# Two units to a matmul in the joins of 32-blocks, with G kept as its off-diagonal half

## Chip, cores, metric

One core of a Trainium2 chip. The time is the device time of the kernel in microseconds (us); each quoted time is a median of several executions. The kernel runs in fp32.

Words used below: PE is the matrix engine, DVE the vector engine, ACT the scalar engine, POOL the GpSimd engine. In this kernel PE's results go to PSUM; a copy or product that takes a result out of it is called an evacuation. Names that begin with ps are buffers in PSUM: psJ the joins, psG the Gram matrices, psK, psQ, psU, psY and psS the other small products of the recurrence, psT and psX transposes, psH and psO the feed-forward. In the profile every fp32 matmul is two instructions. The granted clock is the share of PE's full clock that the chip's throttle let through; half clock is 0.5.

## The reference, cut to what matters

A gated delta rule for 4 batches of 8 heads, 768 steps and head size 48, then a feed-forward block with exact GELU.

```python
for t in range(S):                                   # S = 768
    kt, vt, bt = k_n[:, :, t], v[:, :, t], beta[:, :, t, None]
    y[:, :, t] = einsum('bhd,bhde->bhe', q[:, :, t], state)
    v_old = einsum('bhde,bhd->bhe', state, kt)
    state = state + bt[..., None] * einsum('bhd,bhe->bhde', kt, vt - v_old)
h = y_as_rows @ w_in                                 # 3072 x 384 @ 384 x 2048
out = gelu_exact(h) @ w_out                          # 2048 x 384
```

## The kernel before

The recurrence runs in chunks of 64 steps. Two chunks make a group (there are six), and inside a group every 64x64 triangular system is solved in two steps: its two 32x32 diagonal blocks are inverted by elimination on DVE, for all 32 units (4 tiles of 8 heads) at once, and the off-diagonal 32x32 block then follows from two small products, the *joins* (level 0 and level 1). A unit has two halves p, in partitions 0-63 and 64-127. C is 64, HB is 32.

```python
def products(u, part=(0, 1)):                # Gram matrix of a chunk, 64x64 for each head
    ...
        nc.scalar.copy(heads(Gs[g][:, u.t]), psG[:, :, :, 0:C])          # G, whole, ACT
    ...                                                                  # P on DVE, from psG too
def pack(u, copy=nc.scalar.copy):            # the diagonal blocks in one piece, ACT
    ...
    copy(Ds[g][:, span], Gs[g][:, u.t, :, 0:HB])
    for p in range(2):                       # lower: partitions 32-63 of half p
        copy(Ds[g][lower, span], Gs[g][lower, u.t, :, HB:C])

def join(g, ts, level, copy=nc.scalar.copy):
    ...
    for i, u in enumerate(us):               # 16 units a call (8 in the start), p = 0 and 1
        for p in range(2):
            if level == 0:
                nc.tensor.matmul(psJ[low_, 0, col], lhsT=raw[top, u, HB:C],
                                 rhs=xm[top, u, :], start=True, stop=True)
            else:
                nc.tensor.matmul(psJ[top, 0, col], lhsT=xm[low_, u, :],
                                 rhs=zf[low_, u, HB:C], start=True, stop=True)
    for p in range(2):                       # two evacuations a call
        if level == 0:
            nc.vector.tensor_tensor(xm[low_, span, :], src, gm[...], op=ALU.mult)   # DVE
        else:
            copy(zf[top, span, HB:C], src)                                          # ACT
```

The start (group 0, first half) is scheduled by hand: elimination, joins, first solve. In the main part only DVE's order is fixed by hand; feed-forward matmuls (psH, psO) are laid between the small ones.

Of the kernel before, what the change touches and what calls it, by code (L numbers as in the profile page):

```python
# [8 lines left out]
F32 = mybir.dt.float32  # L9
U32 = mybir.dt.uint32  # L10
AX = mybir.AxisListType
ALU = mybir.AluOpType
# [4 lines left out]
def kernel(  # L17
# [28 lines left out]
    nc = tc.nc  # L46
    B, H, S, D = q.shape
    DM, DF = moe_w_in.shape
    C = 64
    HB = 32  # L50
    NC = S // C
    NP = H // 2
    NA = B // 2
    NG = NC // 2
    NU = 2 * NA * H
    NM = DM // 128
    NF = DF // 128
    HALF = [slice(0, C), slice(C, 2 * C)]
# [4 lines left out]
    wk = ctx.enter_context(tc.tile_pool(name="wk", bufs=2))  # L63
    ps = ctx.enter_context(tc.tile_pool(name="ps", bufs=2, space=bass.MemoryType.PSUM))
    start = ExitStack()
    su = start.enter_context(tc.tile_pool(name="su", bufs=2))

    def dn(name):
        return ps.tile([128, 2, 512], F32, tag="dn", name=name)
# [25 lines left out]
    for c in range(NC):  # L95
        for a in range(NA):
            u = tiles[c, a] = Unit()
# [53 lines left out]
    Zf = [cpool.tile([128, NU, C], F32, name=f"Zf{i}") for i in range(2)]  # L151
# [67 lines left out]
    Ds, Gs, Nus, XMs, gms, ns = {}, {}, {}, {}, {}, {}  # L219

    def heads(ap):
        return ap.rearrange("q (j r) d -> q r j d", r=2)
# [63 lines left out]
    def products(u, part=(0, 1)):  # L286
        g = u.c // 2
        cols = slice(part[0] * C, (part[-1] + 1) * C)
        psG = dn("psG").rearrange("q r (j n) -> q r j n", j=NP)
        for j in range(NP):  # L290
            for r, p in QUADS:
                rows = slice(r * C, r * C + D)
                nc.tensor.matmul(psG[HALF[p], r, j, cols], lhsT=u.KQt[rows, j, p, 0, :],  # L293
                                 rhs=u.KQt[rows, j, p].rearrange("q x n -> q (x n)")[:, cols],
                                 start=True, stop=True)
        if 0 in part:
            if u.t == 0:
                Gs[g] = wk.tile([128, 2 * NA, H, C], F32, tag="G", name="G", bufs=1)
            if u.t == 0 and g > 0:
                Ds[g] = wk.tile([128, NU, HB], F32, tag="diag", name="diag", bufs=1)  # L300
            nc.scalar.copy(heads(Gs[g][:, u.t]), psG[:, :, :, 0:C])  # L301
        if 1 in part:
            u.P = wk.tile([128, H, C], F32, tag="P", name="P", bufs=6)
            if u.c < 2:
                nc.scalar.copy(heads(u.P), psG[:, :, :, C:])
            else:
                nc.vector.tensor_tensor(heads(u.P), psG[:, :, :, C:], heads(mask_h), op=ALU.mult)  # L307

    def pack(u, copy=nc.scalar.copy):
        g = u.c // 2  # L310
        span = slice(u.t * H, (u.t + 1) * H)
        copy(Ds[g][:, span], Gs[g][:, u.t, :, 0:HB])
        for p in range(2):
            lower = slice(p * C + HB, (p + 1) * C)
            copy(Ds[g][lower, span], Gs[g][lower, u.t, :, HB:C])

    def masked(u, engine=nc.gpsimd):
        engine.tensor_tensor(u.P, u.P, mask_h, op=ALU.mult)

    def gram(u):  # L320
        products(u)
        pack(u)

    def diagonals(u):

# [13 lines left out]
    def eliminate_steps(g):  # L339
# [48 lines left out]
        steps += [(1.9, back, x) for x in range(3)]  # L388
        return steps

    def join(g, ts, level, copy=nc.scalar.copy):

        xm, zf, raw = XMs[g], Zf[g % 2], Gs[g].rearrange("q t h n -> q (t h) n")
        gm = gms[g].rearrange("q t h -> q (t h)")
        psJ = dn("psJ")
        us = range(ts[0] * H, (ts[-1] + 1) * H)
        span = slice(us[0], us[-1] + 1)
        for i, u in enumerate(us):
            for p in range(2):
                top = slice(p * C, p * C + HB)  # L400
                low_ = slice(p * C + HB, (p + 1) * C)
                col = slice(i * HB, (i + 1) * HB)
                if level == 0:
                    nc.tensor.matmul(psJ[low_, 0, col], lhsT=raw[top, u, HB:C],  # L404
                                     rhs=xm[top, u, :], start=True, stop=True)
                else:
                    nc.tensor.matmul(psJ[top, 0, col], lhsT=xm[low_, u, :],  # L407
                                     rhs=zf[low_, u, HB:C], start=True, stop=True)
        for p in range(2):
            top = slice(p * C, p * C + HB)  # L410
            low_ = slice(p * C + HB, (p + 1) * C)
            rows = top if level else low_
            src = psJ[rows, 0, 0:len(us) * HB].rearrange("q (u n) -> q u n", n=HB)
            if level == 0:
                nc.vector.tensor_tensor(  # L415
                    xm[low_, span, :], src,
                    gm[low_, span].unsqueeze(2).to_broadcast([HB, len(us), HB]), op=ALU.mult)
            else:
                copy(zf[top, span, HB:C], src)

    def gram_steps(c):
        us = [tiles[c, a] for a in range(NA)]
        return [(1.0, fn, u) for fn in (transposed, gram) for u in us]

    def v_steps(c):
        return [(1.0, scale_v, tiles[c, a], nc.vector if c == 2 else nc.gpsimd)
# [2 lines left out]
    def join_steps(g):  # L429
        return [(1.0, join, g, (2 * cc, 2 * cc + 1), level)  # L430
                for level in range(2) for cc in range(2)]
# [174 lines left out]
    for u in first:  # L606
        products(u, (0,))
    for u in first:
        transposed(u, (1,))
        products(u, (1,))  # L610
# [14 lines left out]
    for a in range(NA):  # L625
        join(0, (a,), 0)
    back2[0](*back2[1:])
    for a in range(NA):
        join(0, (a,), 1)
# [21 lines left out]
    def late():  # L651
        start.close()
        more = ctx.enter_context(tc.tile_pool(name="late", bufs=1))
        for i in range(4):
# [7 lines left out]
             at(1.02, 1.1, [(1.0, join, 0, (2, 3), level) for level in range(2)]),  # L662
]
    plan += [at(0.99, 1.0, [(1.0, prep, 2)]), at(1.055, 1.06, [(1.0, finish, 2)]), at(1.6, 1.61, [(1.0, finish, 3)]), at(2.75, 2.76, [(1.0, finish, 4)]), at(1.06, 1.14, gram_steps(2)),
             at(1.12, 1.6, state_steps(1)), at(1.5, 1.51, [(1.0, prep, 3)]),
             at(1.6, 1.75, gram_steps(3)), at(1.75, 2.45, eliminate_steps(1)),
             at(2.5, 2.62, join_steps(1)), at(2.62, 2.97, state_steps(2)),
             at(2.6, 2.61, [(1.0, prep, 4)]), at(2.65, 2.9, gram_steps(4))]
    plan += [at(1.62, 1.63, [(1.0, load, 4)]), at(0.995, 1.0, [(1.0, load_v, 2)])]
    plan += [at(c - 0.4, c - 0.3, v_steps(c)) for c in range(2, NC)]  # L670
# [46 lines left out]
```

## Time and profile before

| | before |
|---|---|
| time, median | 755.48 us (4 runs, 754.54 to 755.74) |
| PE busy | 704.0 us, 93% of the span |
| DVE busy | 376.4 us, 50% |
| ACT busy | 249.4 us, 33% |
| join call, steady part | 1.13 us of PE, 64 instructions |

The shares are averages over stages with different limits; the prediction tells the stages apart and shows the lines. In them the first two numbers of a timeline line are start and duration in us, and in a group's line the numbers after the first bar are busy us and mean ns of one instruction, after the second the idle time ahead of them and who ended it.

### The profile page before, as it was taken

What the parts mean: (1) busy time and instruction counts of PE and PEld (TensorE: products, weight loads), DVE (VectorE), ACT (ScalarE), POOL (GpSimd) and SP (SyncE); (2) the same over time, 40 slices, a digit from 0 to 9 for tenths busy, and PEclk for the clock granted to TensorE, in tenths of its full rate; (3) what the DMA queues carried; (4) which work ended last, traced back from release to release, by engine and by line L of the source; (5) the groups of instructions that cost most, each with busy time, mean ns of one, the idle gap of its engine ahead of it and who ended that gap; (6) DMA issues with size and microseconds to landing.
All of it is one profiled execution on the core that took longest, in us unless ns stands there. A gap on an engine that the chain in (4) does not pass through costs nothing.

```text
span 753.3 us, 19282 instructions
## 1 busy us (share of the span) xinstructions
PE 704.0 (93%) x8532; PEld 508.5 (68%) x8532; DVE 376.4 (50%) x855; ACT 249.4 (33%) x602; POOL 84.7 (11%) x91
## 2 busy tenths in 40 slices
PE   6549786899999999999999999999999999999997
PEld 5347553576687687687587687687687687586774
DVE  6988999996329722329822329822329821210100
ACT  3335633422553134352134352133352132122120
POOL 5051001203110002110012010012020010000000
PEclk9999999998999999999999999999999999999999
DMA  9807544400311101211101211001001000000000
GB/s 150 199 25 206 131 125 129 103 1 19 60 33 23 32 13 32 44 32 23 34 13 32 44 32 23 12 12 23 12 12 23 12 12 2 11 12 1 22 1 21
DMA packets 84515, 32.90 MB, mean 44 GB/s; under 512 B 77328, under 2 KB 80400, under 8 KB 84432
## 3 DMA queue, kind: packets, MB, share of 16 engines
q1 hardware_dynamic: 78384, 26.36, 16.0%
q10 hardware_dynamic: 5952, 5.12, 3.0%
q8 instruction: 67, 1.10, 0.6%
q0 software_dynamic: 96, 0.20, 0.1%
q14 instruction: 16, 0.13, 0.1%
HBM read 26.94 MB, written 4.72 MB: 42 GB/s over the span
## 4 chain that ended last, share of the span: by engine, by line
PE 77%; DVE 19%; issue 2%; DMA 1%; POOL 1%; ACT 0%; ACTq 0%; POOLq 0%; DVEq 0%
PE psO L544 30%; PE psH L535 30%; DVE tmp L359 3%; DVE Nu L361 3%; PE psT L283 2%; PE psG L293 2%; DVE w_e L204 2%; PE psU L470 2%; PE psJ L404 2%; PE psS L509 2%; PE psQ L447 2%; PE psK L447 2%; PE psJ L407 2%; PE psY L493 1%; DVE w_e L194 1%
## 5 line engine op out<-in xcount | busy, mean ns | idle before, releaser
L544 PE MATMUL psO<-w_out_sb,g 128*128 128x384 f32 x768 | 272.9, 500 | 10.2 <-DVE w_out_sb L205 10.2
L535 PE MATMUL psH<-xT,w_in_sb 128*128 128x256 f32 x1152 | 274.9, 388 | 3.4 <-DVE w_in_sb L205 3.0
L535 PEld LDWEIGHTS psH<-xT,w_in_sb 128*128 128x128 f32 x1152 | 213.1, 191 | 37.4 <-DVE w_in_sb L205 3.5
L544 PEld LDWEIGHTS psO<-w_out_sb,g 128*128 128x128 f32 x768 | 140.4, 192 | 97.2 <-DVE w_out_sb L205 15.6
L538 ACT ACTIVATE g<-psH 128x256 f32<-128x256 f32 x192 | 73.5, 383 | 177.4 <-PE psH L535 177.1
L361 DVE TENSOR_TENSOR Nu<-Nu,tmp 128x30 f32<-128x30 f32 (+9 forms) x180 | 61.9, 344 | 6.2
L359 DVE TENSOR_TENSOR tmp<-Nu 128x30 f32<-128x30 f32 (+9 forms) x180 | 61.8, 343 | 5.6
L253 POOL TENSOR_TENSOR n<-n,half 128x16 f32<-128x16 f32 x10 | 29.5, 2947 | 222.6 <-DVE n L242 222.6
L501 DVE TENSOR_TENSOR x<-psY,y 64x192 f32<-64x192 f32 x88 | 31.0, 353 | 42.3 <-PE psY L493 41.4
L307 DVE TENSOR_TENSOR P<-psG,mask 128x512 f32<-128x512 f32 x20 | 13.7, 690 | 72.8 <-ACT G L301 72.7
L512 DVE TENSOR_TENSOR St<-St,psS 128x384 f32<-128x384 f32 x22 | 12.2, 553 | 75.4 <-PE psS L509 75.0
L459 DVE TENSOR_TENSOR W<-psK,V 128x384 f32<-128x384 f32 x22 | 12.2, 555 | 73.6 <-PE psK L447 56.8
L475 ACT COPY U<-psU 64x192 f32<-64x192 f32 x92 | 28.8, 313 | 46.8 <-PE psU L470 46.0
L548 ACT COPY o_sb<-psO 128x384 f32<-128x384 f32 x24 | 11.5, 479 | 89.3 <-PE psO L544 89.3
L293 PE MATMUL psG<-KQt 48*64 48x128 f32 (+1 forms) x896 | 30.4, 286 | 3.9 <-ACT KQt L284 2.7
L522 ACT COPY xT<-psX 128x384 f32<-128x384 f32 x24 | 11.4, 477 | 68.0 <-PE psX L521 67.9
L293 PEld LDWEIGHTS psG<-KQt 48*64 48x64 f32 x896 | 24.9, 157 | 10.6 <-issue 4.8
L284 ACT COPY KQt<-psT 128x512 f32<-128x512 f32 x48 | 26.5, 589 | 9.1 <-PE psT L283 8.6
L383 POOL MEMSET Zf<- 32x512 f32 x23 | 12.2, 529 | 147.5 <-DVE Zf L374 145.5
L404 PE MATMUL psJ<-XM,G 32*32 32x32 f32 x768 | 15.5, 198 | 13.6 <-DVE XM L370 13.6
L415 DVE TENSOR_TENSOR XM<-psJ,gm 32x512 f32<-32x512 f32 (+1 forms) x26 | 16.9, 649 | 20.4 <-PE psJ L404 20.1
L196 ACT ACTIVATE w_e<-w_e,lim 128x384 uint32<-128x384 uint32 (+2 forms) x31 | 19.4, 625 | 23.0 <-DVE w_e L194 22.8
(100 smaller groups left out, 584.9 us busy)
## 6 DMA issues: line engine op xcount, KB each, us to landing
Qp<-in_q_dram SPq DMA_DIRECT2D x48, 96.0 KB, 3.4
V<-in_v_dram SPq DMA_DIRECT2D x48, 96.0 KB, 2.9
w_out_sb<-in_moe_w_in_dram SPq DMA_DIRECT2D x9, 512.0 KB, 5.3
out_dram<-o_sb ACTq DMA_DIRECT2D x48, 96.0 KB, 2.2
Zf<-in_moe_w_out_dram SPq DMA_DIRECT2D x8, 384.0 KB, 3.5
w_raw<-in_moe_w_out_dram SPq DMA_DIRECT2D x8, 384.0 KB, 3.1
Kp<-in_k_dram SPq DMA_DIRECT2D x28, 96.0 KB, 3.1
w_out_sb<-in_moe_w_in_dram SPq DMA_DIRECT2D x6, 256.0 KB, 4.4
```

Source lines behind the costliest of these rows:

```text
L253: nc.gpsimd.tensor_tensor(flat, flat, half, op=ALU.pow)
L284: nc.scalar.copy(u.KQt[:, :, :, x, :], psT.rearrange("q j (p n) -> q j p n", p=2))
L293: nc.tensor.matmul(psG[HALF[p], r, j, cols], lhsT=u.KQt[rows, j, p, 0, :], rhs=u.KQt[rows, j, p].rearrange("q x n -> q (x n)")[:, cols], s ...
L359: nc.vector.tensor_tensor(tmp, nu[:, j + 1:, j:j + 1].to_broadcast([128, n, j]), nu[:, j:j + 1, 0:j].to_broadcast([128, n, j]), op=ALU.mult)
L361: nc.vector.tensor_tensor(nu[:, j + 1:, 0:j], nu[:, j + 1:, 0:j], tmp, op=ALU.add)
L404: nc.tensor.matmul(psJ[low_, 0, col], lhsT=raw[top, u, HB:C], rhs=xm[top, u, :], start=True, stop=True)
L447: nc.tensor.matmul(psum(p, j, r), lhsT=u.KQt[rows, j, p, x, :], rhs=St[rows, u.a, p, j, :], start=True, stop=True)
L475: copies[i % len(copies)](pairs(u.U[HALF[p]], s), pairs(psU[HALF[p ^ s], p], s))
L501: nc.vector.tensor_tensor(dst, src, pairs(u.y[HALF[p ^ s]], s), op=ALU.add)
L535: nc.tensor.matmul(psH, lhsT=w_in_sb[:, m, f * 128:(f + 1) * 128], rhs=xTs[c][:, m, :], start=(m == 0), stop=(m == NM - 1))
L538: nc.scalar.activation(gs[f], psH, ACT.Gelu)
L544: nc.tensor.matmul(u.psO, lhsT=gs[f][:, u.a * 128:(u.a + 1) * 128], rhs=w_out_sb[:, f, :], start=(f == 0), stop=(f == NF - 1))
```

## The change

The intent: put two units side by side into one matmul, so that a join call has half as many. The weights are then 64 columns wide and the stream 64 columns long; the two 32x32 blocks on the diagonal of the 64x64 output are the wanted ones, the other two are waste. The two units' columns have to be merged into one weight operand, and the build refuses that when they do not lie side by side. So G is kept as its off-diagonal half alone and the diagonal blocks are copied straight from PSUM.

```diff
@@ products
-            nc.scalar.copy(heads(Gs[g][:, u.t]), psG[:, :, :, 0:C])
+            nc.scalar.copy(heads(Gs[g][:, span]), psG[:, :, :, HB:C])
+            if g > 0:
+                ...
+                nc.scalar.copy(heads(Ds[g][:, span]), psG[:, :, :, 0:HB])
+                for p in range(2):
+                    lower = slice(p * C + HB, (p + 1) * C)
+                    nc.scalar.copy(Ds[g][lower, span], Gs[g][lower, span])
... (pack and gram are gone)
@@ join
-        for i, u in enumerate(us):
+        for k in range(n):                       # n = half the units
             for p in range(2):
...
+                nc.tensor.matmul(psJ[HALF[p], k, :],
+                                 lhsT=left[rows, u:u + 2, :].rearrange("q u n -> q (u n)"),
+                                 rhs=right, start=True, stop=True)
         for p in range(2):
-            src = psJ[rows, 0, 0:len(us) * HB].rearrange("q (u n) -> q u n", n=HB)
+            for x in range(2):                   # four evacuations a call, half the size
+                src = psJ[p * C + x * HB:p * C + (x + 1) * HB, :, x * HB:(x + 1) * HB]
...
```

More of the change, by code (lines that the diff above doesn't have):

```diff
@@ L297, in products @@
             if u.t == 0:
-                Gs[g] = wk.tile([128, 2 * NA, H, C], F32, tag="G", name="G", bufs=1)
-            if u.t == 0 and g > 0:
-                Ds[g] = wk.tile([128, NU, HB], F32, tag="diag", name="diag", bufs=1)
-            nc.scalar.copy(heads(Gs[g][:, u.t]), psG[:, :, :, 0:C])
+                Gs[g] = wk.tile([128, NU, HB], F32, tag="G", name="G", bufs=1)
+            span = slice(u.t * H, (u.t + 1) * H)
+            nc.scalar.copy(heads(Gs[g][:, span]), psG[:, :, :, HB:C])
+            if g > 0:
+                if u.t == 0:
+                    Ds[g] = wk.tile([128, NU, HB], F32, tag="diag", name="diag", bufs=1)
+                nc.scalar.copy(heads(Ds[g][:, span]), psG[:, :, :, 0:HB])
+                for p in range(2):
+                    lower = slice(p * C + HB, (p + 1) * C)
+                    nc.scalar.copy(Ds[g][lower, span], Gs[g][lower, span])
         if 1 in part:
@@ L307, in products @@
                 nc.vector.tensor_tensor(heads(u.P), psG[:, :, :, C:], heads(mask_h), op=ALU.mult)
-    def pack(u, copy=nc.scalar.copy):
-        g = u.c // 2
-        span = slice(u.t * H, (u.t + 1) * H)
-        copy(Ds[g][:, span], Gs[g][:, u.t, :, 0:HB])
-        for p in range(2):
-            lower = slice(p * C + HB, (p + 1) * C)
-            copy(Ds[g][lower, span], Gs[g][lower, u.t, :, HB:C])
     def masked(u, engine=nc.gpsimd):
         engine.tensor_tensor(u.P, u.P, mask_h, op=ALU.mult)
-    def gram(u):
-        products(u)
-        pack(u)
     def diagonals(u):
@@ L389, in eliminate_steps, with every @@
         return steps
+    def every(ap, x):
+        return ap.rearrange("q (k x) n -> q k x n", x=2)[:, :, x]
     def join(g, ts, level, copy=nc.scalar.copy):
-        xm, zf, raw = XMs[g], Zf[g % 2], Gs[g].rearrange("q t h n -> q (t h) n")
+        xm, zf, off = XMs[g], Zf[g % 2], Gs[g]
         gm = gms[g].rearrange("q t h -> q (t h)")
-        psJ = dn("psJ")
-        us = range(ts[0] * H, (ts[-1] + 1) * H)
-        span = slice(us[0], us[-1] + 1)
-        for i, u in enumerate(us):
+        n = len(ts) * H // 2
+        psJ = dn("psJ")[:, 0, 0:n * C].rearrange("q (k n) -> q k n", n=C)
+        span = slice(ts[0] * H, (ts[-1] + 1) * H)
+        for k in range(n):
+            u = span.start + 2 * k
             for p in range(2):
@@ L401, in join @@
                 low_ = slice(p * C + HB, (p + 1) * C)
-                col = slice(i * HB, (i + 1) * HB)
                 if level == 0:
-                    nc.tensor.matmul(psJ[low_, 0, col], lhsT=raw[top, u, HB:C],
-                                     rhs=xm[top, u, :], start=True, stop=True)
-                else:
-                    nc.tensor.matmul(psJ[top, 0, col], lhsT=xm[low_, u, :],
-                                     rhs=zf[low_, u, HB:C], start=True, stop=True)
+                    rows, left, right = top, off, xm[top, u:u + 2, :]
+                else:
+                    rows, left, right = low_, xm, zf[low_, u:u + 2, HB:C]
+                nc.tensor.matmul(psJ[HALF[p], k, :],
+                                 lhsT=left[rows, u:u + 2, :].rearrange("q u n -> q (u n)"),
+                                 rhs=right, start=True, stop=True)
         for p in range(2):
@@ L411, in join @@
             low_ = slice(p * C + HB, (p + 1) * C)
-            rows = top if level else low_
-            src = psJ[rows, 0, 0:len(us) * HB].rearrange("q (u n) -> q u n", n=HB)
-            if level == 0:
-                nc.vector.tensor_tensor(
-                    xm[low_, span, :], src,
-                    gm[low_, span].unsqueeze(2).to_broadcast([HB, len(us), HB]), op=ALU.mult)
-            else:
-                copy(zf[top, span, HB:C], src)
+            for x in range(2):
+                src = psJ[p * C + x * HB:p * C + (x + 1) * HB, :, x * HB:(x + 1) * HB]
+                if level == 0:
+                    nc.vector.tensor_tensor(
+                        every(xm[low_, span, :], x), src,
+                        gm[low_, span].rearrange("q (k x) -> q k x", x=2)[:, :, x:x + 1]
+                        .to_broadcast([HB, n, HB]), op=ALU.mult)
+                else:
+                    copy(every(zf[top, span, HB:C], x), src)
     def gram_steps(c):
         us = [tiles[c, a] for a in range(NA)]
-        return [(1.0, fn, u) for fn in (transposed, gram) for u in us]
+        return [(1.0, fn, u) for fn in (transposed, products) for u in us]
     def v_steps(c):
```

## The prediction

> **What bounds the kernel now.** I read the page's slices first, then busy time by stage (windows), the chain of waits for each stage, the groups by shape, and last the starts of single matmuls in the trace.
>
> ```profile
> PE   6549786899999999999999999999999999999997
> DVE  6988999996329722329822329822329821210100
> ```
>
> Each digit is a slice of 18.8 us. Up to the ninth slice (about 170 us) DVE is nearly full and PE is not; after that PE is full. The windows say it in numbers (PE, PEld, DVE, ACT, POOL busy):
>
> ```profile
> 0.00:60.00 60.00, 33.20 (x882) 27.68 (x882) 47.41 (x123) 20.89 (x44) 19.48 (x34) 1.00 0.62 130
> 60.00:143.00 83.00, 67.78 (x778) 45.10 (x771) 79.75 (x176) 40.90 (x88) 8.52 (x8) 0.97 0.52 134
> 143.00:171.00 28.00, 26.14 (x129) 21.13 (x129) 25.66 (x67) 7.09 (x18) 1.92 (x1) 0.97 0.20 42
> 378.00:660.00 282.00, 281.59 (x3518) 203.36 (x3518) 112.50 (x248) 90.51 (x226) 27.41 (x24) 1.00 0.09 18
> ```
>
> So there are three regimes: a start in series (0 to 60 us), a DVE-bound stretch (79.75 of 83 us busy, then the elimination of group 1) and from 171 us a PE-bound stretch, in which only PE time counts. The chain of waits agrees: it runs through DVE lines to 170.7 us, then through PE without a hole. The change touches ACT copies (hidden in all three regimes: ACT is busy 90.5 of 282 us in the steady part), join matmuls (on the path from 171 us) and the joins' evacuations (on the path only in the start and the DVE stretch).
>
> The steady part, timeline of PE:
>
> ```profile
> 264.45 1.20 PE L404 MATMUL psJ<-XM,G 32*32 32x32 f32 x64
> 265.58 2.86 PE L535 MATMUL psH<-xT,w_in_sb 128*128 128x256 f32 x12
> 268.36 1.20 PE L404 MATMUL psJ<-XM,G 32*32 32x32 f32 x64
> 269.49 1.56 PE L535 MATMUL psH<-xT,w_in_sb 128*128 128x256 f32 x6
> 270.99 1.20 PE L407 MATMUL psJ<-Zf,XM 32*32 32x32 f32 x64
> 272.12 2.86 PE L535 MATMUL psH<-xT,w_in_sb 128*128 128x256 f32 x12
> ```
>
> A join call occupies PE from 264.45 to 265.58, 1.13 us for 64 instructions (32 matmuls; every fp32 matmul of this trace is two instructions). Feed-forward matmuls lie between a join and its use.
>
> **What the Trainium skill says.** (1) "TensorEngine Tiling (Array Packing)", Instruction Overhead: a matmul with one moving column has the same latency as one with 60. If that floor bound the joins, half the matmuls at twice the columns would halve their time. The trace disagrees: the psJ instructions start in pairs (one for each p, 6 or 7 ns apart), and pairs follow every 31.5 ns; 2 passes x 32 columns at 2.4 GHz are 26.7 ns. The pair is paced by its columns, not by a floor. (2) "TensorE: Matmul & The Clock Gate", LDWEIGHTS: the load takes a time set by its columns, not its rows. The trace agrees: psK (48 rows, 64 weight columns, 48 moving) starts its rounds of four every 58.8 ns, longer than 2 x 48 / 2.4 = 40 ns of streaming, and close to 2 x 64 / 2.4 = 53 ns of weights; psG with the same weights and 128 moving columns has rounds of 109 ns, and 2 x 128 / 2.4 = 107. So a round takes the longer of weights and stream, plus 2 to 5 ns. (3) "FP8 and Floating Point Precision", TensorE Precision Notes: true fp32 is four passes, which fits two instructions of two passes each.
>
> **The change, part by part.**
>
> *Join matmuls.* Two units side by side give 64 weight columns, 64 moving columns, 32 rows; half the output is waste. A call becomes 16 matmuls, 32 instructions, still in two tiles (p = 0 and 1), so 16 rounds instead of 32. By (1) and (2) each round is the larger of 53 ns (weights) and 53 ns (stream) plus about 5, call it 59 ns, against 31.5. First start to last: before 53 + 30 x 31.5 + 7 = 1.01 us (the trace: 1.009). After 95 (the first gap of psK is 93) + 14 x 59 + 7 = 0.93 us. From the last start to the next block's first: 121 ns for psJ (32 moving), 148 for psK (48), 199 for psG (128), hence about 158 for 64. The call: 0.93 + 0.16 = 1.09 instead of 1.13 us, 0.04 us less. On the PE-bound path lie 4 calls for each of five groups: 20 x 0.04 = 0.8 us. Group 1's calls partly run at half rate (pairs every 53 ns), where the same argument gives nothing more; I allow 0.1. **Minus 0.9 us.**
>
> *Evacuations of the joins.* Each becomes two of half the size. From the groups by shape:
>
> ```profile
> L415 DVE TENSOR_TENSOR XM<-psJ,gm 32x512 f32<-32x512 f32 x22 | 15.2, 690 | 20.3 <-PE psJ L404 20.1
> L415 DVE TENSOR_TENSOR XM<-psJ,gm 32x256 f32<-32x256 f32 x4 | 1.7, 424 | 0.1
> L419 ACT COPY Zf<-psJ 32x512 f32<-32x512 f32 x22 | 12.7, 575 | 19.2 <-PE psJ L407 19.0
> L419 ACT COPY Zf<-psJ 32x256 f32<-32x256 f32 x4 | 1.4, 362 | 0.1
> ```
>
> DVE: (690 - 424) / 256 = 1.04 ns an element and 158 ns fixed; ACT 0.83 and 149. So 2 x 690 becomes 4 x 424 on DVE (0.32 us more for a call), 2 x 575 becomes 4 x 362 on ACT. In the steady part both are hidden: psJ of level 0 ends at 265.6, its two evacuations end near 267, and level 1 reads them at 270.99, 4 us later. In the DVE-bound stretch one call (group 0, second half) pays: **plus 0.3 us.**
>
> In the start nothing hides them:
>
> ```profile
> 44.44 1.75 DVE L415 TENSOR_TENSOR XM<-psJ,gm 32x256 f32<-32x256 f32 x4
> 46.23 1.93 DVE L374 STREAM_TRANSPOSE Zf<-Nu 128x1024 f32<-128x1024 f32 x1
> 48.26 0.63 ACT L381 ACTIVATE Zf<-low 32x512 f32<-32x512 f32 x1 [16.57 <-DVE Zf L374]
> 48.90 1.49 ACT L419 COPY Zf<-psJ 32x256 f32<-32x256 f32 x4
> 49.73 1.96 PE L470 MATMUL psU<-W,Zf 64*64 64x48 f32 x64 [2.32 <-DVE w_in_sb L197]
> ```
>
> This is a series: four DVE products, the transpose, the zeroing on ACT, two of the four copies (they end at 49.63), then psU. Its stated releaser is a DVE line, but psU starts 0.1 us after the second copy and reads what it writes. Four products of 0.437 us pitch (1.75) become eight of 128 elements: 158 + 133 = 291 ns, pitch about 0.31, 2.45 us: plus 0.7. Two copies (0.74) become four of 149 + 106 = 255 ns, pitch 0.27, 1.07 us: plus 0.33. **Plus 1.0 us** for everything behind. The join matmuls of the start are slower there (pairs of 53 ns) and finish under the second transpose, 42.5 to 44.4; twice the columns in half the rounds keeps that.
>
> *Gram copies.* A unit from chunk 2 on costs ACT 584 (G) + 404 + 2 x 402 (diag, the small ones being 32 partitions) = 1.79 us; afterwards two PSUM reads of 256 columns, 372 each (the psD copy of the same shape), and 2 x 402 = 1.55 us. That is 0.24 x 20 = 4.8 us of ACT, and 0.84 us in the four units of group 0, but no wait in the chain ends on these copies except 1.9 us in all before the flip transposes, and there the POOL product with the scales (143.29 to 145.21) ends after the transpose anyway. **0 us.** The freed half of G (4 KB in each partition) is not missing anywhere.
>
> Sum: 1.0 + 0.3 - 0.9 = +0.4 us on 755.7, so **756.1 us**.
>
> **Rivals.** (a) The joins are bound by instruction count: 1.13 would become about 0.62 us, 20 x 0.5 = 10 us less, 745. For it: 17.7 ns an instruction is the lowest pitch of any group, and psK with its 32 instructions occupies 0.61 us. Against it: the 31.5 ns rounds of two, while psG and psK issue four in 20 ns. (b) The two wide tiles no longer run together (64 weight columns for 32 rows occur nowhere in this trace): 32 x 56 ns = 1.8 us a call, plus 0.7 x 20 = 14 us, 769. For it: only that the shape is new; against it: four 64-column tiles run together in psK, and p = 0 and 1 share no rows and no output partitions. (c) The four evacuations hold back level 1 or the next user of psJ's buffer: the slack of 4 us speaks against it; if it were a wait of 0.5 us at 20 calls, 766. (d) The main part fixes by hand only DVE's order, so other durations can move ACT and PE work against each other; that is worth a few us either way, and I cannot work it out.
>
> **Range and chances.** The sum is made of terms of at most 1 us, runs of before spread over 1.2 us, and (d) adds perhaps 2 to 3 us: 753.0 to 759.5. To leave 2% the time must move by 15 us: (a) falls short of it, (b) just misses. Faster 0.01, same 0.97, slower 0.02.
>
> **What would show it.** Right: join calls at 1.05 to 1.12 us in the steady part, rounds of two near 58 ns; psU at 50.6 to 50.9 instead of 49.73 and group 1's first join about 1.3 us after 170.7; the end less than 1 us after that of before. Wrong: join calls near 0.6 or 1.8 us (rivals a, b), idle PE before psJ of level 1 (c), or a different order of PE blocks between 171 and 707 us (d).

## The result and the profile after

The changed kernel took 756.61 us (median of 4 runs, 756.29 to 756.78), predicted 756.1. Ratios here are the mean time of one kernel's fast runs over the mean of the other's in the same rounds, so they are not quite the ratio of the medians; for this one it is 1.0017 (95% interval 0.9999 to 1.0034). In a second set with more rounds it was 1.0021 (0.9999 to 1.0043). Both intervals still hold no change at all, so the times alone do not size an effect this small. All outputs are right.

Where the trace of the changed kernel stands against that of the kernel before (starts in us, read from the timelines):

| event | before | changed | shift |
|---|---|---|---|
| XM transpose that ends the first elimination | 40.57 | 41.00 | +0.43 |
| first psU | 49.73 | 51.13 | +1.40 |
| first psH | 60.06 | 61.66 | +1.59 |
| elimination of group 1 begins | 142.95 | 145.48 | +2.54 |
| first join of group 1 | 170.70 | 173.22 | +2.52 |
| psK after the joins of group 1 | 181.15 | 183.07 | +1.93 |
| first join of group 5 | 605.09 | 606.57 | +1.48 |
| end | 753.30 | 754.57 | +1.27 |

The start and the DVE-bound stretch lose 2.5 us; 0.6 us come back between the first join of group 1 and the psK after it, and 0.66 us from there to the end. The 0.6 us cannot be put down to the joins: over all traces this piece takes 9.90 to 10.45 us with old joins (the kernel before, kernels 2 and 8 below) and 9.85 to 10.20 us with new ones (the changed kernel twice, kernel 1). Half clock falls into it. In the kernel before it began 1.25 us after the first join and lay on a busy PE all the time; in the changed kernel its first 0.93 us fell on an idle PE.

**The joins in the steady part.** PE's timeline, changed kernel:

```profile
266.38 1.15 PE L406 MATMUL psJ<-XM,G 32*64 32x64 f32 x32
267.45 2.86 PE L536 MATMUL psH<-xT,w_in_sb 128*128 128x256 f32 x12
270.24 1.15 PE L406 MATMUL psJ<-XM,G 32*64 32x64 f32 x32
271.32 1.56 PE L536 MATMUL psH<-xT,w_in_sb 128*128 128x256 f32 x6
```

Half the instructions (x32), nearly the same time: from a call's first start to the next block's first start it is 1.077 us, before 1.130. The pairs of instructions (p = 0 and 1) start every 58.4 ns instead of every 31.7.

**The evacuations.** Groups by shape, changed kernel:

```profile
L415 DVE TENSOR_TENSOR XM<-psJ,gm 32x256 f32<-32x256 f32 x44 | 18.5, 421 | 18.9 <-PE psJ L406 18.4
L420 ACT COPY Zf<-psJ 32x256 f32<-32x256 f32 x44 | 16.0, 363 | 19.2 <-PE psJ L406 18.7
L415 DVE TENSOR_TENSOR XM<-psJ,gm 32x128 f32<-32x128 f32 x8 | 2.3, 288 | 0.1
L420 ACT COPY Zf<-psJ 32x128 f32<-32x128 f32 x8 | 2.0, 256 | 0.1
```

Twice as many, at 421 and 288 ns on DVE instead of 690 and 424, so each halving costs what the fixed part of an instruction costs. In the start that shows, all engines' timeline of the changed kernel (lines between left out):

```profile
44.87 2.42 DVE L415 TENSOR_TENSOR XM<-psJ,gm 32x128 f32<-32x128 f32 x8
47.31 1.92 DVE L368 STREAM_TRANSPOSE Zf<-Nu 128x1024 f32<-128x1024 f32 x1
49.33 0.63 ACT L375 ACTIVATE Zf<-low 32x512 f32<-32x512 f32 x1 [16.40 <-DVE Zf L368]
49.97 2.14 ACT L420 COPY Zf<-psJ 32x128 f32<-32x128 f32 x8
51.13 2.14 PE L471 MATMUL psU<-W,Zf 64*64 64x48 f32 x64 [2.58 <-ACT Zf L420]
```

The eight products take 2.42 us where four took 1.75, and psU starts 1.16 us after the first copy instead of 0.83. Its releaser is now named as the ACT copy, which fits the reading that the DVE releaser named before was only the last semaphore seen.

**The DVE-bound stretch** lost 0.95 us (from +1.59 to +2.54), of which two more evacuations (four of 0.42 for two of 0.69) explain 0.3. Most of the rest is one wait. DVE's timeline, first the kernel before, then the changed one:

```profile
95.73 0.69 DVE L205 SCALAR_TENSOR_TENSOR w_in_sb<-w_in_sb,w_e 128x512 f32<-128x512 f32 x1
96.34 0.68 DVE L204 SCALAR_TENSOR_TENSOR w_e<-w_out_sb,w_e 128x512 uint32<-128x512 uint32 x1
```

```profile
97.65 0.69 DVE L205 SCALAR_TENSOR_TENSOR w_in_sb<-w_in_sb,w_e 128x512 f32<-128x512 f32 x1
98.90 0.69 DVE L204 SCALAR_TENSOR_TENSOR w_e<-w_out_sb,w_e 128x512 uint32<-128x512 uint32 x1 [0.56 <-ACT w_e L196]
```

DVE waits 0.56 us for an ACT step of the weight decoding. In ACT's timeline copies that wait for PE stand ahead of that step. So the question is why PE was late. The windows point to its clock (PE, PEld, DVE, ACT, POOL busy in us; then the mean granted clock of PE, here the number after the last bracket), kernel before, then changed:

```profile
80.00:83.00 3.00, 3.00 (x37) 2.08 (x37) 2.93 (x7) 1.38 (x3) 0.00 (x0) 0.50 0.93 230
83.00:87.00 4.00, 4.00 (x54) 2.96 (x54) 3.83 (x8) 1.93 (x5) 0.00 (x0) 0.97 0.81 105
```

```profile
80.00:83.00 3.00, 1.46 (x4) 1.17 (x4) 2.93 (x7) 0.21 (x1) 0.00 (x0) 0.52 0.46 120
83.00:87.00 4.00, 4.00 (x40) 2.79 (x38) 3.86 (x8) 1.17 (x3) 0.00 (x0) 0.51 1.16 214
```

In both kernels PE falls to half clock near 80 us, before for 3.4 us, in this run of the changed kernel for 6.8 us (the clock records of the trace give the lengths). Whether that belongs to the change is a question for the experiments.

**The gram copies** left a trace that I had not predicted. DVE's mask product P reads the same PSUM tile as ACT's copies and waits for them; from the page of each kernel, before and then changed:

```profile
L307 DVE TENSOR_TENSOR P<-psG,mask 128x512 f32<-128x512 f32 x20 | 13.7, 690 | 72.8 <-ACT G L301 72.7
```

```profile
L313 DVE TENSOR_TENSOR P<-psG,mask 128x512 f32<-128x512 f32 x20 | 13.7, 690 | 73.5 <-ACT diag L304 73.5
```

It now waits for the second of two copies of 256 columns (370 and 377 ns, overlapping a little), which ends about 0.06 us later than the one copy of 512 (584 ns). Behind P on DVE come the products x, and PE waits for those before one transpose; PE's timeline, before and then changed:

```profile
319.36 0.55 PE L521 MATMUL psX<-ident,x 128*128 128x128 f32 x3 [0.21 <-DVE x L501]
```

```profile
321.14 0.55 PE L522 MATMUL psX<-ident,x 128*128 128x128 f32 x3 [0.27 <-DVE x L502]
```

This occurs in three of the groups: 3 x 0.06 = 0.2 us. It closes the account of the steady part: 16 calls x 0.053 = 0.85 us won, 0.2 lost, 0.65 net; from psK to the end the table has 1.93 - 1.27 = 0.66.

### The profile page after: what moved, and what is told of

Same layout as the page of the kernel before. It is cut to its first block, busy times and chain, and to the rows that moved or that the text cites. A ratio compares the mean times of both kernels' runs of the same rounds, so it can differ in the third digit from the quotient of the medians.

```text
span 754.6 us, 17817 instructions
## 1 busy us (share of the span) xinstructions
PE 703.3 (93%) x7764; PEld 507.9 (67%) x7764; DVE 381.0 (50%) x881; ACT 245.8 (33%) x628; POOL 84.4 (11%) x91
## 4 chain that ended last, share of the span: by engine, by line
PE 78%; DVE 17%; issue 1%; ACT 1%; DMA 1%; SPq 0%; POOL 0%; ACTq 0%; DVEq 0%; POOLq 0%
PE psH L536 30%; PE psO L545 30%; PE psJ L406 3%; DVE tmp L353 3%; DVE Nu L355 3%; PE psT L283 2%; PE psU L471 2%; PE psG L293 2%; PE psQ L448 2%; PE psK L448 2%; PE psS L510 2%; DVE w_e L204 2%; PE psY L494 1%; DVE w_out_sb L199 1%; PE psX L522 1%
## 5 line engine op out<-in xcount | busy, mean ns | idle before, releaser
L415 DVE TENSOR_TENSOR XM<-psJ,gm 32x256 f32<-32x256 f32 (+1 forms) x52 | 20.8, 401 | 19.1 <-PE psJ L406 18.4
L406 PE MATMUL psJ<-XM,G 32*64 32x64 f32 x384 | 16.0, 243 | 14.1 <-DVE XM L364 14.1
```

Of the source, the lines that this page charges most:

```text
L406: nc.tensor.matmul(psJ[HALF[p], k, :], lhsT=left[rows, u:u + 2, :].rearrange("q u n -> q (u n)"), rhs=right, start=True, stop=True)
```

## The experiments

Theory: a round of matmuls (one in each tile that works at the time; a tile here is a block of PE's rows and columns that holds one small weight matrix) takes the longer of its weight load and its stream, so wide matmuls save almost nothing; the start pays for halved evacuations; the rest is small. Eight kernels were run, in two sets of four, each set beside its own runs of the kernel before (11 runs, median 755.55 us in the first set, 753.69 in the second; why these differ is found below).

### 1. The start undone

```diff
@@ start only; join_one is the join of before, on the new G
-        join(0, (a,), 0)
+        join_one(0, (a,), 0)
...
-        join(0, (a,), 1)
+        join_one(0, (a,), 1)
```

> The changed kernel, but the four join calls of the start (group 0, first half) again with one unit to a matmul and two evacuations a call. My theory: the start pays about 1.0 us for the halved evacuations, nothing else of it changes, so psU starts about 1.0 us earlier than in the changed kernel and the time is about 755.6 us (1.0 below the changed kernel's 756.6). Rival (the halved evacuations cost nothing, the longer start comes from other order or from waits before the joins): no change, 756.6 us.

Measured: 755.23 us (5 runs, 754.69 to 756.42), ratio to before 1.0002 (0.9989 to 1.0014). PE's timeline:

```profile
49.55 1.96 PE L501 MATMUL psU<-W,Zf 64*64 64x48 f32 x64 [2.33 <-DVE w_in_sb L197]
```

From the first XM transpose to psU it is 9.17 us, as in the kernel before (9.16) and not as in the changed kernel (10.13). The rival falls. A steady join call still takes 1.077 us.

### 2. The gram copies alone

```diff
@@ from the changed kernel: every join as before, on the new G (in short; join's whole body is replaced)
-    def join(...)      # two units to a matmul
+    def join(...)      # one unit to a matmul, two evacuations, lhsT=off[top, u, :]
```

> Only the gram copies of the change (G kept as its off-diagonal half, diagonal blocks copied straight from PSUM); all joins with one unit to a matmul and two evacuations. My theory: ACT busy falls by about 5.6 us to some 244, nothing on the path moves: 755.5 us, within 0.4 of the kernel before. Rival (the new ACT durations move waits: the 0.4 us that psD waits in the start of the changed kernel and the 0.6 us that DVE waits there for ACT's decode near 98 us): 756.3 to 756.6 us.

Measured: 754.75 us (5 runs, 754.45 to 756.93), ratio 0.9999 (0.9985 to 1.0014). ACT busy fell by 7.0 us to 242.4, more than I had worked out. The lines behind it, groups by shape of this run:

```profile
L300 ACT COPY G<-psG 128x256 f32<-128x256 f32 x24 | 8.9, 371 | 31.5 <-PE psG L293 31.5
L304 ACT COPY diag<-psG 128x256 f32<-128x256 f32 x20 | 7.6, 378 | 0.0
```

Two PSUM reads of 256 columns stand in place of one of 512 and one SBUF copy. The durations of all these copies sum to 5.6 us less than before (38.2 to 32.6), as worked out; neighbouring ones now also overlap, by 2.0 us in all, and ACT's other work took 0.6 us more. In the time, nothing shows (the interval allows about 1 us either way), and DVE does not wait near 97 us in this trace, so the rival finds no support; what that wait goes with is found below. But psX waits 0.27 us at 319 us here as well, and from psK to the end this run loses 0.18 us to the trace of before, the 0.2 us of the account above. So the gram copies cost about 0.2 us by the traces (0.3 in kernel 8, which has them and the old joins there too); the timing cannot resolve it.

### 3. Four tiles at once

```diff
@@ join, from kernel 1: one unit to a matmul again, x = 0, 1 go to different column groups
-            for p in range(2):
+            for x, p in ((0, 0), (0, 1), (1, 0), (1, 1)):
...
-                nc.tensor.matmul(psJ[HALF[p], k, :],
-                                 lhsT=left[rows, u:u + 2, :].rearrange("q u n -> q (u n)"),
-                                 rhs=right, start=True, stop=True)
+                nc.tensor.matmul(psJ[p * C + x * HB:p * C + (x + 1) * HB, k, 0:HB],
+                                 lhsT=left[rows, u + x, :], rhs=right[:, x, :],
+                                 start=True, stop=True)
...
-                src = psJ[p * C + x * HB:p * C + (x + 1) * HB, :, x * HB:(x + 1) * HB]
+                src = psJ[p * C + x * HB:p * C + (x + 1) * HB, :, 0:HB]
```

> Start as before; in all other join calls one unit to a matmul (32 weight columns, 32 moving), but the two units of a pair write to different column groups, so that four 32x32 tiles work at once; 64 instructions a call as before the change, four half-size evacuations as in the change. My theory (a round is paced by 2 x 32 columns, 31.5 ns, however many tiles are in it): 16 rounds, a call takes 53 + 14 x 31.5 + 20 + 121 = 0.64 us instead of 1.13 (before) and 1.08 (changed), so 20 x 0.44 = 9 us below the first run of this set, about 747 us. Rival (the count of instructions binds, 17.7 ns each): a call stays at 1.13 us, about 756.5 us.

Measured: 749.13 us (6 runs, 746.31 to 750.29), ratio 0.9917 (0.9899 to 0.9936). PE's timeline:

```profile
264.81 0.75 PE L406 MATMUL psJ<-XM,G 32*32 32x32 f32 x64
265.50 2.86 PE L566 MATMUL psH<-xT,w_in_sb 128*128 128x256 f32 x12
```

The same 64 instructions of the same shape as before the change, in 0.682 us a call instead of 1.130: the count of instructions does not bind, the number of tiles at work does. The gain was smaller than expected (6.1 us below kernel 1 by the medians, not 9). A call was 0.04 us longer than worked out, because after the first half of it the starts no longer come in fours every 31.7 ns but in twos every 17 ns; so the 16 calls of groups 2 to 5 give 6.3 us. And group 1's four, partly at half clock, gave almost nothing (9.95 us from its first join to psK, 10.20 in kernel 1).

### 4. Wide weights, narrow stream

```diff
@@ join, from kernel 1: 32 matmuls a call, x and p as in kernel 3
+                wide = left[rows, u:u + 2, :].rearrange("q u n -> q (u n)")
+                nc.tensor.matmul(psJ[HALF[p], k, x * HB:(x + 1) * HB], lhsT=wide,
+                                 rhs=right[:, x, :], start=True, stop=True)
```

> Start as before; in all other calls the weights are two units wide (64 columns) but each matmul streams only one unit (32 columns), 32 matmuls a call, two tiles a round. My theory (a round takes the longer of weights and stream): rounds of 59 ns set by the weights, a call 95 + 30 x 59 + 7 + 121 = 2.0 us, 20 x 0.92 = 18 us above the first run of this set, about 774 us. Rival (only the stream paces a round, the weights are hidden): rounds of 31.5 ns, a call 1.13 us, about 756.7 us.

Measured: 777.01 us (4 runs, 775.88 to 780.61), ratio 1.0296 (1.0274 to 1.0318). PE's timeline:

```profile
276.15 2.05 PE L407 MATMUL psJ<-XM,G 32*64 32x32 f32 x64
278.14 2.86 PE L566 MATMUL psH<-xT,w_in_sb 128*128 128x256 f32 x12
```

The stream is that of the kernel before, only the weights are wide, and a call takes 1.98 us; pairs start every 58.4 ns, as in the changed kernel. So 64 weight columns alone set that pace. The profiled run is the slowest one (780.61 us, 6.6 above expectation), and 6 us of that lie in group 1: there PE ran at half clock for 23.9 us (6.8 in the kernel before), and the four calls took 14.0 us together instead of about 8. Why the other three runs (775.88 to 777.33) lie 2 to 3 us above expectation no trace shows.

### 5. Narrow weights, wide stream

```diff
@@ join, from kernel 1: 32 matmuls a call, four tiles as in kernel 3
+                nc.tensor.matmul(psJ[p * C + x * HB:p * C + (x + 1) * HB, k, :],
+                                 lhsT=left[rows, u + x, :], rhs=right,
+                                 start=True, stop=True)
```

> The mirror of the run with wide weights: start as before; in all other calls the weights are one unit (32 columns), each matmul streams two units (64 columns), the two units of a pair in different column groups (four tiles a round, 64 instructions a call). My theory (a round takes the longer of weights and stream): rounds of four at 59 ns set by the stream, a call 1.08 us as in the changed kernel, time as in the run with only the start undone, about 755.5 us. Rival (the weights alone made the changed kernel's rounds long, the stream is hidden): rounds as in the four-tile run, a call 0.68 us, about 749 us.

Measured: 756.65 us (4 runs, 755.56 to 757.10), ratio 1.0027 (1.0007 to 1.0046). PE's timeline:

```profile
266.44 1.09 PE L406 MATMUL psJ<-XM,G 32*32 32x64 f32 x64
267.46 2.86 PE L566 MATMUL psH<-xT,w_in_sb 128*128 128x256 f32 x12
```

Rounds of four start every 56 ns, a call takes 1.03 us against 0.68 with the narrow stream. So 64 streamed columns alone also set nearly that pace. Kernels 4 and 5 together show "the longer of the two": both wide together (the changed kernel, 58.4 ns) is no slower than the weights alone, and either one was enough to take back what the halved count gave. The time missed its forecast by 1.1 us, although the calls were shorter than forecast; in the profiled run group 1 took 12.4 us from its first join to psK (10.2 in kernel 1), with half clock for 10.2 us in place of 6.8.

### 6. Four tiles, group 0 as before

```diff
@@ plan, from kernel 3
-             at(1.02, 1.1, [(1.0, join, 0, (2, 3), level) for level in range(2)]),
+             at(1.02, 1.1, [(1.0, join_one, 0, (2, 3), level) for level in range(2)]),
```

> The four-tile kernel, but all joins of group 0 (start and second half, in the DVE-bound stretch) with one unit and two evacuations as before. Two theories of the 0.9 to 1.6 us by which the DVE-bound stretch was longer in all runs with the new joins there: (A) it is the new join at 63 to 70 us: 0.3 us of evacuation, and a PE that is a little less busy there, so that the half-clock stretch at 80 us lasts 6.8 to 10.2 us instead of 3.4 and DVE waits for ACT near 97 us; then this run has one 3.4 us half-clock stretch there and starts the elimination of group 1 within 0.3 us of the kernel before, and ends about 1 us before the four-tile run, 748 us. (B) the length of the half-clock stretch is chance: then 6.8 us or more may come again and the time stays about 749 us.

Measured: 748.28 us (6 runs, 745.67 to 750.05), ratio 0.9912 (0.9891 to 0.9934), the lowest median of all, though the ratio does not tell it from kernel 3. But theory A falls as the sole cause. The half-clock stretch lasted 6.8 us here too, with the old join in its place, and DVE waited again, DVE's timeline:

```profile
97.23 0.69 DVE L204 SCALAR_TENSOR_TENSOR w_e<-w_out_sb,w_e 128x512 uint32<-128x512 uint32 x1 [0.80 <-ACT w_e L196]
```

### 7. The changed kernel again

Unaltered, no diff.

> The changed kernel unaltered, in more rounds and beside the others: 756.6 us, 0.5 to 1.5 us above the kernel before. If the half-clock stretch near 80 us is due to the new join there it lasts 6.8 us again; if it is chance it may be 3.4 us, with DVE not waiting near 98 us and a time about 0.6 us lower.

Measured: 756.42 us (6 runs, 753.84 to 758.77), ratio 1.0021 (0.9999 to 1.0043). In the profiled run the half-clock stretch lasted 6.8 us and DVE waited 1.17 us. DVE's timeline:

```profile
99.00 0.69 DVE L204 SCALAR_TENSOR_TENSOR w_e<-w_out_sb,w_e 128x512 uint32<-128x512 uint32 x1 [1.17 <-ACT w_e L196]
```

The +0.43 us at the end of the first elimination did not come again (the XM transpose starts 0.08 us earlier than in the kernel before), so that part of the first comparison was chance.

### 8. The new joins in the start alone

```diff
@@ from the changed kernel
-        return [(1.0, join, g, (2 * cc, 2 * cc + 1), level)
+        return [(1.0, join_one, g, (2 * cc, 2 * cc + 1), level)
... (and the second half of group 0 likewise)
```

> The counterpart of the run with the start undone: new joins in the start alone, one unit to a matmul everywhere else, gram copies as in the change. My theory: psU starts at 50.7 us instead of 49.7 and everything behind it 1.0 us later; the joins' saving of about 0.9 us is missing: 756.5 us. Rival (the longer start is taken up by waits of the DVE-bound stretch): 755.5 us.

Measured: 756.78 us (6 runs, 756.48 to 757.74), ratio 1.0032 (1.0016 to 1.0047). All engines' timeline:

```profile
44.44 2.41 DVE L415 TENSOR_TENSOR XM<-psJ,gm 32x128 f32<-32x128 f32 x8
50.71 1.50 PE L501 MATMUL psU<-W,Zf 64*64 64x48 f32 x40 [2.60 <-ACT Zf L420]
```

Here the series begins at 44.44 us, exactly where it begins in the kernel before, so the comparison is clean: psU comes at 50.71 instead of 49.73, 0.98 us later. The rival falls.

### The half clock over all runs

The profiled runs sort themselves by the length of the half-clock stretch near 80 us. With 3.4 us (the kernel before, kernels 2 and 5) or none there (kernel 4) DVE does not wait near 97 us; with 6.8 us or more (the changed kernel twice, kernels 1, 3, 6, 8) it waits 0.5 to 1.2 us. Both lengths occur with old joins there and with new ones, so the join alone does not decide it. Near 171 us, where group 1's joins begin, every profiled run has a second stretch: 6.8 us in the kernel before, the changed kernel twice and kernels 1, 2 and 8, 10.2 us in kernels 3, 5 and 6, 23.9 us in kernel 4. The timed runs of one kernel mostly sort themselves in the same way by their mean granted clock: the kernel before took 753.40 to 753.47 us at 0.993 and 755.17 to 756.08 at 0.989. That is why its median differed between the two sets, and it gives the cleanest estimate of the change that the record allows. At equal clock, 0.992: changed 753.84 and 754.20, before 753.25, 753.42 and 753.69, difference 0.57 us. At 0.988: changed 756.24, 756.48, 756.69 and 756.74, before 755.68, 755.95 and 756.09, difference 0.63 us. At equal clock, then, the change costs about 0.6 us. Two limits belong to this figure. The mean clock is a rough key: it also counts half clock after the last matmul (in the kernel before from 752.2 us on; the matmuls end at 749.0), at 0.991 the kernel before took 753.05 as well as 754.29 us, and one run of kernel 6 at 0.954 took 748.20, no longer than others. And it leaves out what the change may do to the clock itself: eight of ten runs of the changed kernel had 0.988 or less, four of 22 of the kernel before. Whether the change brings long stretches more often is not shown, and what decides how long a half-clock stretch lasts in a given run stays open.

## Why the prediction was right, point by point

- **The joins' matmuls**: predicted 1.09 us a call and rounds near 59 ns, measured 1.077 and 58.4. The reason, the longer of weights and stream, was shown for each side alone (kernels 4 and 5). One step of the argument was weaker than it looked: pairs of 32 columns every 31.7 ns could not by themselves tell a floor from columns; that 64 columns take 56 to 58 ns can. (Its readings of 31.5 and 58.8 ns, the latter for psK, are 31.7 and 58.3 in the trace.) The 2 / 2.4 ns a column of its sums is borne out by the trace before: psH with 256 columns starts every 215.8 ns and psO with 384 every 322.5, 0.833 ns a column. The saving was 0.053 us a call rather than 0.04, because from the last start to the next block it is 147 ns, not 158. The 16 calls of groups 2 to 5 saved 0.85 us where 0.64 was counted, and the 0.26 us counted for group 1 cannot be seen (two calls at half clock: 3.61 us with the new joins, 3.55 with the old). The total of 0.9 came out by two errors that cancel.
- **The start**: predicted 1.0 us, measured 0.98 (kernel 8), and undoing it brings psU back (kernel 1). The mechanism, the fixed part of more evacuations, was right.
- **The evacuations in the DVE-bound stretch**: predicted 0.3; four of 0.42 us for two of 0.69 are 0.3, and in kernels 4 and 5, which have the four evacuations and no DVE wait, the way from the first psH to group 1's first join is 0.4 and 0.3 us longer than before. The larger shift of group 1 that the first trace showed (2.5 us, predicted 1.3) is that, 0.4 us of chance before the joins, and a DVE wait that comes with a longer half-clock stretch. I had not foreseen that this stretch differs from run to run.
- **The gram copies**: predicted 0, and this step failed, by a little. I had looked for waits on the copies only before the flip transposes and overlooked the row of P, whose 72.7 us of waits name ACT's copy of G. It cost about 0.2 us.
- **Rival (a)**, bound by count, fell with kernel 3, which has the old count in 60% of the time. **Rival (b)**, wide tiles that do not run together, fell with the pairs of the changed kernel, 6 to 7 ns apart. **Rival (c)**, level 1 waiting for the evacuations, was not seen: no join of the steady part waits. **Rival (d)**: all 266 blocks of PE from 264 us to the end stand in the same order in both traces.

- **The signs it named**: call time and rounds came. psU at 50.6 to 50.9 came in the repeat (50.63) and in kernel 8, not in the first trace (51.13). Group 1's first join "about 1.3 us" later and an end "less than 1 us" later came in neither trace of the changed kernel (2.5 and 2.6 us; 1.27 and 1.63 us), because of the half-clock stretch.

The sum of 0.4 us stands against 0.6 at equal clock: 0.2 us of gram copies was missing, start and evacuations were right within 0.1, and the joins were right in total only. That the time itself came within 0.5 us of the forecast is partly luck: the medians of the kernel before alone lie between 753.69 and 755.55 us in three sets.

## What to carry to other kernels

Count small matmuls in rounds, not in instructions: read the starts of the single ones, see how many tiles work at once, and ask whether weights or stream pace a round. If only two of the tiles work, filling the other column groups (0.68 us a call here) pays, and widening the matmuls with waste does not. A form of output that needs more, smaller evacuations costs its fixed part wherever nothing hides it, which is in the start; keep the old form there. When runs of one kernel differ by more than the effect sought, compare runs of the same granted clock, and look in the traces where the half clock fell.

## What the Trainium skill lacked or had wrong

- "TensorEngine Tiling (Array Packing)", Instruction Overhead: its floor of about 60 cycles, with the same latency for 1 and for 60 columns, would make an fp32 matmul of 32 columns nearly as dear as one of 64, if it is read by the operand's columns. With four tiles the rounds were 31.7 ns at 32 columns at first and 56 ns at 64 (kernels 3 and 5). The page lacks how fp32 counts against the floor: here each further column cost 0.833 ns in each of a matmul's two instructions.
- "TensorE: Matmul & The Clock Gate", LDWEIGHTS: columns alone count, which the trace bears out (64 columns in 32 rows pace a round at 58.4 ns, estimate by its formula 53). It lacks the rule for a stream of small fp32 matmuls in tiles: a round takes the longer of weights and stream (kernels 4 and 5).
- The same page, Part 1: half clock in windows of about 3.4 us fits the trace (stretches of 3.4, 6.8, 10.2 and 23.9 us). It puts the ramp penalty at under 1% of a typical span; between runs of one kernel it moved the time by 0.3% here (753.4 us at a mean clock of 0.993, 755.6 at 0.989). It lacks the warning that this is enough to cover a change of 0.6 us, and that the mean granted clock also counts half clock after the last matmul.
- "PSUM — Partial Sum Buffer", Terms: two engines must not read one bank at once. DVE's P starts only when ACT's last read of the tile has ended (0.06 us later after two copies than after one); no run let the two read together. The page lacks what follows: splitting one reader's copy delays the other reader.
